# Attention and a mixture of experts on one core: another order and other tile shapes in attention, one output tile that spans the end of each expert's arm, branches announced earlier

## The chip, the core and the metric

The kernel runs on one core of a Trainium2 chip. The core has a matrix engine (TensorE, PE in the profile, with its weight loads as PEld), VectorE (DVE), ScalarE (ACT), GpSimd (POOL) and SyncE (SP, which here only issues transfers). Each engine works through its own instructions in the order in which they were written and waits at semaphores for the others. The metric is the device time of one execution in microseconds (us), lower is better.

## What is computed

`q`, `k`, `v` are 8 batches x 8 heads x 576 positions x 64, all float32. The attention is causal with a decay: each position `s` adds `max(s, 0)` to a running sum, and the difference of two running sums is taken off a score. The heads of a position side by side are a row of 512 numbers, 4608 rows in all. Each row goes to the one expert (of 8) with the largest gate logit.

```python
scores = scale * np.matmul(q, k.transpose(0, 1, 3, 2))
cum = np.cumsum(np.maximum(s, 0.0), axis=-1)
bias = -(cum[:, :, :, None] - cum[:, :, None, :])
scores = np.where(causal, -1000000000.0, scores + np.minimum(bias, 0.0))
attn = np.exp(scores - np.max(scores, axis=-1, keepdims=True))
attn = attn / (np.sum(attn, axis=-1, keepdims=True) + 1e-09)
x = np.matmul(attn, v)            # then rows of 8 heads x 64 = 512
...
e_idx = np.argmax(x @ w_gate, axis=1)
for e in range(E):
    mask = e_idx == e
    h = np.maximum(x[mask] @ w1[e], 0.0)          # 512 -> 1024
    ye = h @ w2[e]                                # 1024 -> 512
    out[mask] = gate_w[mask, None] * eom[mask, e, None] * ye
```

`gate_w` is the softmax weight of the chosen expert, `eom` a sigmoid of a second gate.

## The kernel before

**Attention.** The work goes by pairs of heads: 32 pairs, two heads of 64 side by side in the 128 partitions. Of a pair, q and k are transposed on PE (`trans`, lines 302 and 306) and copied to SBUF (`k_copy`, `q_copy`). The 576 rows of scores are five tiles t = 0..4: four of 128 rows, where tile t needs (t+1)*128 columns, and tile 4, the last 64 rows of both heads, 576 columns. `scores` (line 381) multiplies with 64 rows of the array for each head, so that two heads run side by side. For tile 4 (line 384) each head's 64 rows use one quarter of the array, 64 x 64; the columns are done in two halves of 288, so that two of the four quarters are used. GpSimd writes the decay and the mask into SBUF (`bias`: line 350 for t < 4, 356 and 363 for tile 4, 360 the mask); DVE adds the scores from PSUM and takes the row minimum in one instruction (`least`, line 397, the signs are turned); ACT takes exp and the row sum (`expo`, line 417); PE transposes the result 128 columns at a time (`ptrans`, line 427; the last 64 columns of tile 4 in `ptail`, line 453); ACT or DVE copies it to SBUF (`copy`, lines 310 and 312); PE multiplies by v (`av`, lines 471 and 473, two heads side by side by columns). The result goes through `ocopy` and `xout` (lines 501 and 502: a transpose and the gate logits) and is scaled on DVE (line 514) and stored.

**Banks.** [...] Two are one tile `A` (k, and the product with v); six are one pool, tag `S`, that scores (two banks a tile), transposes, q and `xout` take in turn. A bank is free again when DVE or ACT has read it.

**The order** is made by a planner (`Order`): each piece of work has a place `pos`, an engine, a cost in ns and what it must come after; the planner lets the engines run through these costs and writes each engine's instructions in the order that results. `LAG` is what it adds from an engine's end to another's start, `TURN` what it adds on PE when the shape into which the array is divided changes (0: the whole array; 1: two halves of 64 rows; 2: quarters; 3: two halves of 64 columns). These numbers only set the order.

**Experts.** The last pairs run beside the first expert's early rows (three tiles `ET` of 128 rows gathered from the batches before the last, and two tiles of output `EY`, `early_gemm2`). How many rows an expert has is known only on the chip (`count`, read by every engine in `arm_of`). For each expert there is a switch with one arm per size, 512 to 768 rows in steps of 32 (`front`), and behind the switch code common to all arms (`back`). `hint` lets every engine announce the branch, so that the arm's instructions are fetched ahead. Weights and activations are split into a high and a low float32r part, and a product takes three multiplications (lines 772 and 810). In an arm: h for all eight blocks of 128 (`gemm1`, PSUM tile `ph`, two buffers), then output tile 0 and tiles 4 and above (`gemm2`, PSUM tile `py`, two buffers; 24 multiplications, then DVE scales it into `y`, line 1053, and GpSimd scatters it). A last tile of 32 or 64 rows is done in `gemm2_few` (line 1076). In `back`: output tiles 1, 2, 3 (tile 2 alone for expert 0), between them the transposes of the next expert's gathered rows (`ready`, line 749, with copies `xh` on ACT and `xl` on DVE, line 757), and in the last quarter of tile 3 the hint. If an expert has more than 640 rows, its sixth tile is transposed at the start of the arm (`ready(LT, ...)`).

## Time and profile before

| | |
|---|---|
| median of 3 runs | 912.95 us (912.15 to 914.6) |
| the profiled execution's own time | 906.76 us |
| its span, first to last instruction | 904.9 us |
| mean granted TensorE clock | 0.992 |
| busy: PE, PEld | 858.5 us (95%), 646.5 us (71%) |
| busy: DVE, ACT, POOL | 460.7 us (51%), 444.1 us (49%), 488.1 us (54%) |
| HBM read, written | 102.73 MB, 19.95 MB |

Times in the trace are us from the span's start. A row of a table by stretches has, for each stretch, busy time and number of instructions of each engine, then the granted TensorE clock, the share of the 16 transfer engines in use and GB/s. A row of waits reads: engine and line, `<-` what it waited for, us in total, times, the longest. A row of the chain of waits reads: start, us until the next piece, what ran. A float32 multiplication of two tiles is two instructions (two passes) on PE, a transpose is one.

### The profile page before, as it was taken

The numbers are of one execution on the slowest core, as the hardware profiler recorded it, in microseconds if no ns is written. First come the engines' busy times: TensorE is split into PE (matmuls) and PEld (weight loads), VectorE is DVE, ScalarE is ACT, GpSimd is POOL, SyncE is SP. The second block draws the span as 40 slices with busy tenths as digits, with TensorE's granted clock in tenths as the row PEclk, the third lists the DMA queues.
The fourth block names the chain that finished last, engine by engine and source line by source line (L and its number), as shares of the span: only waits on it lengthen the run. The fifth ranks groups of instructions, "written<-read, shape, count | busy, mean of one in ns | idle before, by whom it ended". The sixth has DMA issues, their size and how long they took to land.

```text
span 904.9 us, 16965 instructions
## 1 busy us (share of the span) xinstructions
PE 858.5 (95%) x5574; PEld 646.5 (71%) x5574; DVE 460.7 (51%) x1274; ACT 444.1 (49%) x1128; POOL 488.1 (54%) x854
## 2 busy tenths in 40 slices
PE   3999999999999999999988989999999999999996
PEld 2656666666666666666877768779779787897985
DVE  4666656575667656676724443536135135352210
ACT  2678777777777778778412514233033042331300
POOL 7685867678686867675551443626135126262401
PEclk9999999999999999999989999999999999999999
DMA  8997687969799697922345361532612615424001
GB/s 184 186 208 178 132 182 147 214 153 204 179 184 207 147 205 160 187 58 73 111 125 170 91 231 57 175 123 70 215 50 59 218 45 157 146 71 137 16 14 51
DMA packets 169449, 124.91 MB, mean 138 GB/s; under 512 B 128650, under 2 KB 147084, under 8 KB 169230
## 3 DMA queue, kind: packets, MB, share of 16 engines
q1 hardware_dynamic: 161150, 100.50, 45.9%
q0 software_dynamic: 8080, 22.08, 8.0%
q8 instruction: 65, 1.06, 0.5%
q14 instruction: 154, 1.26, 0.5%
HBM read 102.73 MB, written 19.95 MB: 136 GB/s over the span
## 4 chain that ended last, share of the span: by engine, by line
PE 79%; issue 9%; POOL 4%; DMA 3%; DVE 2%; SPq 1%; another core or an unknown queue 1%; ACT 0%; POOLq 0%; DVEq 0%; ACTq 0%
PE py L810 17%; PE ph L772 16%; PE PT L427 10%; PE S L381 10%; PE A L473 9%; PE S L384 4%; PE M L501 3%; PE M L502 2%; PE pt L749 2%; PE Aq L306 2%; PE A L306 1%; POOL w L707 1%; PE A L471 1%; PE py L1076 1%; POOL xg L739 1%
## 5 line engine op out<-in xcount | busy, mean ns | idle before, releaser
L810 PE MATMUL py<-w,hh 128*128 128x512 f32 x420 | 133.9, 400 | 7.4 <-DVE y L1053 5.1
L1033 POOL DMA_INDIRECT out_dram<-y,tb x34 | 33.6, 989 | 195.1 <-DVE y L1053 173.5
L427 PE MATMUL PT<-ident,e 128*128 128x128 f32 x768 | 112.8, 280 | 0.6 <-DVE kq L325 0.6
L772 PE MATMUL ph<-xh,w1h 128*128 128x512 f32 (+6 forms) x312 | 104.9, 336 | 6.3 <-issue 4.7
L772 PE MATMUL ph<-xl,w1h 128*128 128x512 f32 (+6 forms) x312 | 103.7, 332 | 4.4 <-DVE xl L757 4.4
L381 PE MATMUL S<-kq 64*128 64x384 f32 (+3 forms) x512 | 104.5, 489 | 1.3 <-ACT kq L323 1.3
L772 PE MATMUL ph<-xh,w1l 128*128 128x512 f32 (+6 forms) x312 | 103.6, 332 | 0.0
L427 PEld LDWEIGHTS PT<-ident,e 128*128 128x128 f32 x768 | 86.4, 144 | 21.4 <-ACT e L417 9.6
L753 ACT CAST xh<-pt 128x512 fp32r<-128x512 f32 x37 | 21.6, 587 | 153.0 <-PE pt L749 147.3
L810 PEld LDWEIGHTS py<-w,hh 128*128 128x128 f32 x420 | 76.7, 189 | 25.5 <-DVE y L1053 7.6
L310 ACT COPY pt<-PT 128x512 f32<-128x512 f32 (+3 forms) x170 | 82.6, 513 | 20.5 <-PE PT L427 19.5
L473 PE MATMUL A<-pt,vraw 128*64 128x448 f32 (+3 forms) x640 | 90.1, 416 | 0.0
L350 POOL TENSOR_SCALAR pbB<-cb,cumt 128x384 f32<-128x384 f32 (+1 forms) x128 | 59.9, 478 | 49.0 <-ACT e L417 33.4
L810 PE MATMUL py<-w,hl 128*128 128x512 f32 x210 | 82.6, 393 | 0.0
L1053 DVE TENSOR_SCALAR y<-py,tb 128x512 f32<-128x512 f32 x33 | 24.8, 751 | 107.3 <-PE py L810 96.2
L721 DVE TENSOR_TENSOR w1l<-w1r,w1h 128x512 fp32r<-128x512 f32 x44 | 50.9, 1156 | 53.1 <-ACT w1h L718 52.9
L473 PEld LDWEIGHTS A<-pt,vraw 128*64 128x64 f32 (+1 forms) x640 | 41.8, 136 | 45.0 <-issue 36.1
L417 ACT ACTIVATE e<-pbA,m 128x512 f32<-128x512 f32 x64 | 46.3, 723 | 56.3 <-DVE m L397 54.2
L772 PEld LDWEIGHTS ph<-xh,w1h 128*128 128x128 f32 x312 | 59.7, 191 | 12.9 <-issue 6.9
L784 DVE SCALAR_TENSOR_TENSOR hl<-ph,hh 128x512 fp32r<-128x512 f32 (+6 forms) x72 | 50.5, 702 | 34.6 <-ACT hh L782 34.5
L417 ACT ACTIVATE e<-pbB,m 128x384 f32<-128x384 f32 (+1 forms) x128 | 64.6, 506 | 5.3 <-DVE m L397 5.3
L772 PEld LDWEIGHTS ph<-xl,w1h 128*128 128x128 f32 x312 | 59.8, 192 | 7.8 <-DVE xl L757 5.2
(171 smaller groups left out, 1907.9 us busy)
## 6 DMA issues: line engine op xcount, KB each, us to landing
cb<-cumd SPq DMA_DIRECT2D x62, 432.0 KB
w1r<-in_moe_w_dram SPq DMA_DIRECT2D x7, 2048.0 KB
w2r<-in_moe_w_dram SPq DMA_DIRECT2D x7, 2048.0 KB
raw<-in_k_dram SPq DMA_DIRECT2D x64, 128.0 KB
raw<-in_q_dram SPq DMA_DIRECT2D x64, 128.0 KB
vraw<-in_v_dram SPq DMA_DIRECT2D x64, 128.0 KB
xd<-x SPq DMA_DIRECT2D x32, 256.0 KB
w1r<-in_moe_w_dram SPq DMA_DIRECT2D x4, 512.0 KB
```

What stands on the lines that cost most here:

```text
L310: nc.scalar.copy(out, in_)
L350: nc.gpsimd.tensor_scalar(pb, st[i]["cb"][:, j, 0:W], 1.0, cumt[:, t, 2 * i + j:2 * i + j + 1], ALU.mult, ALU.add)
L381: nc.tensor.matmul(d["s", t, j][:, 0:width(t)], qt[js, t * P:(t + 1) * P], kt[js, 0:width(t)], start=True, stop=True)
L384: nc.tensor.matmul(d["s", t, n][js, 0:H], d["ql"][js], kt[js, n * H:(n + 1) * H], start=True, stop=True)
L417: nc.scalar.activation(e[:, o:o + W], pbias(i, t, j), AF.Exp, bias=st[i].pop(("m", t, j)), scale=-1.0, accum_out=sums[i % 3][:, j, t:t + 1])
L427: nc.tensor.transpose(p[:, (c * len(g) + n) * P:(c * len(g) + n + 1) * P], st[i][etile(t, j)][:, o:o + P], ident)
L473: nc.tensor.matmul(p[j * D:(j + 1) * D, OB + q0:OB + S], vt[0:kk, j, c, :], pt[0:kk, c, j, q0:S], start=(c == 0), stop=(c == NM))
L721: eng.tensor_sub(w1f("l", f), w1r[:, :, f * P:(f + 1) * P], w1f("h", f).bitcast(F32))
L772: nc.tensor.matmul(p[:, u, 0:W], w1f(a, f)[:, c, :], wt[b_][:, c, us], start=(n == 0), stop=(n == 3 * ND - 1))
L784: nc.vector.scalar_tensor_tensor(lv, pv, 0.0, hv.bitcast(F32), ALU.max, ALU.subtract)
L810: nc.tensor.matmul(p[0:m], wt[a][:, f, sl], w2f(b_, f), start=(f == 0 and n == 0), stop=(f == NF - 1 and n == 2))
L1033: ins = nc.gpsimd.indirect_dma_start(out=dst, out_offset=bass.IndirectOffsetOnAxis(ap=ix, axis=0), in_=y, in_offset=None, bounds_check=dst ...
```

## The change

**Attention, tile 4.** The 64 rows of a head's last tile now take 64 + 256 = 320 columns in each of two halves of the partitions: the lower half the own 64 columns (the only ones that need a mask) and columns 0..255, the upper half columns 192..511, of which the first 64 are masked out. So tile 4 has two parts like the others (j = the head), every one of its four multiplications uses another quarter of the array, and the two heads write different banks. k is laid out with its last 64 columns first, and the running sums get a second layout in DRAM (`cumd`) and in `cb` (1792 instead of 1728 columns). Its row minimum is now taken of two halves: two small copies on ACT (`other_least`) and a minimum on DVE (`both_least`); `sum_move` and `rsum` add the two halves' sums (one more small DVE operation). Two exps of 320 columns take the place of one of 576, two transposes the place of one in `ptail`, two bias operations of 320 the place of one of 576.

**Attention, order.** New places, costs, lags and turn costs; scores only after their bias is written and after the pair before has transposed the same tile. `SLACK` is 40 instead of 250 and the turn cost depends on the shape. The order that the planner then writes is another one. Of the load of the first expert's weights, each piece is issued three pairs earlier.

**Experts.** The first output tile of an expert gets a bank of its own (`pf`). Six of its eight blocks (`FB`) are multiplied in the arm, in pieces ahead of, between and behind the arm's other tiles, the last two behind the end of the arm; `py` has one buffer instead of two, and tile 2 of `back` uses `pf`. The hint stands ahead of tile 3 (of tile 2 for expert 0) instead of in its last quarter; the first expert's hint comes six blocks into the first early output tile. An arm with a sixth tile multiplies the first half of its columns for two blocks ahead.

```diff
-GROUPS = (((3, 0),), ((0, 0), (0, 1)), ((3, 1),), ((2, 0),), ((4, 0),), ((2, 1),), ((1, 0), (1, 1)))
+GROUPS = (((3, 0),), ((0, 0), (0, 1)), ((2, 1),), ((4, 0), (4, 1)), ((1, 0), (1, 1)), ((2, 0),), ((3, 1),))
+BURSTS = ((3,), (0,), (2,), (4,), (1,))
-TURN = 95
+TURN = (95, 200, 125, 150)
-    SLACK = 250
-    LAG = {"PE": 300, "ACT": 250, "DVE": 480, "POOL": 340, "SP": 2300}
+    SLACK = 40
+    LAG = {"PE": 170, "ACT": 370, "DVE": 560, "POOL": 510, "SP": 2300}
...
         for a in range(2):
-            nc.sync.dma_start(cumd[:, a, 0:2, :].rearrange("i j s -> i (j s)"), cum)
-        nc.sync.dma_start(cumd[:, :, 2, :], cum)
+            nc.sync.dma_start(cumd[:, a, 0:2 * S], cum)
+            c4 = cumd[:, a, 2 * S:].rearrange("i (j w) -> i j w", j=2)
+            if a:
+                nc.sync.dma_start(c4, cum[:, H - TL:2 * H])
+            else:
+                nc.sync.dma_start(c4[:, :, 0:TL], cum[:, 2 * H:S])
+                nc.sync.dma_start(c4[:, :, TL:], cum[:, 0:H])
...
-        H = S // 2
-        for n in parts(t):
+        for a in range(1 if t < NM else 2):
             for j in range(2):
                 js = slice(j * D, (j + 1) * D)
...
-                    nc.tensor.matmul(d["s", t, n][js, 0:H], d["ql"][js], kt[js, n * H:(n + 1) * H],
+                    nc.tensor.matmul(d["s", t, j][a * D:(a + 1) * D, 0:W4], d["ql"][js], kt[js, a * H:a * H + W4],
                                      start=True, stop=True)
...
+    def other_least(i):
+        d = st[i]
+        d["mo"] = sm.tile([P, 2], F32, tag="mo", name="mo")
+        for a in range(2):
+            nc.scalar.copy(d["mo"][a * D:(a + 1) * D], d["mt"][(1 - a) * D:(2 - a) * D])
+
+    def both_least(i):
+        d = st[i]
+        nc.vector.tensor_tensor(d["mt"], d["mt"], d["mo"], ALU.min)
...
-        nc.tensor.transpose(p[0:TL, 0:P], st[i]["e4"][:, NM * P:S], ident)
+        for j in range(2):
+            nc.tensor.transpose(p[0:TL, j * P:(j + 1) * P], st[i]["e4"][:, j * W4:j * W4 + TL], ident)
...
-    add("hint", o + 53.0, "PE", 400, hint_first, after=["count", ("g2", EY - 1, 0)])
+    add("hint", o + 43.0, "PE", 400, hint_first, after=["count", ("g2", 0, 1)])
...
+        ahead = range(2) if T > LT and C - c0 > 512 else ()
+        for f in ahead:
+            gemm1(f, c0, C, block(f), 0)
         for f in range(NF):
...
+        first = 0 if e else ET
+        f0 = 2 if few else 0
+        if f0:
+            product2(first, P, firsts[e], range(f0))
         for k, t in enumerate(tiles):
...
+            if k + 1 < len(tiles):
+                product2(first, P, firsts[e], range(f0, f0 + 1))
+                f0 += 1
+        product2(first, P, firsts[e], range(f0, FB))
...
         if e == 0:
-            where = {EY: ((0, 1), (2,), (3,), (4, "hint"))}
+            where = {EY: (("hint", 0, 1), (2,), (3,), (4,))}
         else:
-            where = {1: ((),), 2: ((0,), (1,)), 3: ((2,), (3,), (4,), ("hint",))}
+            where = {1: ((),), 2: ((0,), (1,)), 3: (("hint", 2), (3,), (4,), ())}
+        first = 0 if e else ET
+        product2(first, P, firsts[e], range(FB, NF))
+        result(e, first, P, firsts[e])
```

In the rows that follow, a number behind a tile's name is its buffer, `xN` stands for so many equal instructions, and the size is that of what is written. `S` are scores (`kq` holds k and q), `PT` the transposes of the exp tiles (`e30` and `e31`: tile 3 of head 0 and 1; `e20`, `e21`: tile 2; `e4`, `e1`, `e0`), `A` the product with v or the transpose of k, `M` the output of `xout`.

PE in the middle of attention, from one product with v back to the transposes ahead of it, before:

```order
L427 MATMUL PT_1642<-ident_80,e20_1514 128x128 x3
L302 MATMUL A_1650<-ident_80,raw_1274 128x128
L306 MATMUL A_1650<-ident_80,raw_1274 128x128 x4
L427 MATMUL PT_1663<-ident_80,e4_1544 128x128 x4
L427 MATMUL PT_1677<-ident_80,e21_1553 128x128 x3
L381 MATMUL S_1682<-kq_1458 128x384
L381 MATMUL S_1683<-kq_1458 128x384
L384 MATMUL S_1694<-kq_1458 64x288 x2
L384 MATMUL S_1695<-kq_1458 64x288 x2
L427 MATMUL PT_1707<-ident_80,e1_1557 128x128 x4
L427 MATMUL PT_1722<-ident_80,e30_1622 128x128 x4
L381 MATMUL S_1734<-kq_1458 128x256
```

The same place with the change:

```order
L314 MATMUL A_2077<-ident_80,raw_1658 128x128
L319 MATMUL A_2077<-ident_80,raw_1658 128x128 x4
L448 MATMUL PT_2088<-ident_80,e20_2052 128x128 x3
L448 MATMUL PT_2100<-ident_80,e31_2005 128x128 x4
L396 MATMUL S_2113<-kq_1895 64x320
L396 MATMUL S_2114<-kq_1895 64x320
L396 MATMUL S_2113<-kq_1895 64x320
L396 MATMUL S_2114<-kq_1895 64x320
L393 MATMUL S_2139<-kq_1895 128x512
L393 MATMUL S_2140<-kq_1895 128x512
L393 MATMUL S_2156<-kq_1895 128x128
L393 MATMUL S_2157<-kq_1895 128x128
```

The scores, which stood singly between transposes, now stand together: tile 4, then tiles 3 and 0 of the next pair, in front of the product with v, and tiles 1 and 2 behind it.

PE at the end of an arm of the first expert and the start of the code behind it, before:

```order
L810 MATMUL py<-w_6930,hh 128x512 x2
L810 MATMUL py<-w_6930,hl 128x512
L810 MATMUL py<-w_6935,hh 128x512 x2
L810 MATMUL py<-w_6935,hl 128x512
L1211 UNCONDITIONAL_BRANCH
L852 TENSOR_LOAD rgi
L749 MATMUL pt<-ident,xg 128x128 [waits DMASW3_49,DMASW0_49,PE_49]
L749 MATMUL pt<-ident,xg 128x128 x3
L749 MATMUL pt<-ident,xg 128x128 [waits DMASW5_49,DMASW4_49,DMASW1_49]
L749 MATMUL pt<-ident,xg 128x128 x3
L810 MATMUL py<-w_6843,hh 128x512 [waits DVE_49]
```

With the change:

```order
L1273 UNCONDITIONAL_BRANCH
L877 TENSOR_LOAD rgi
L835 MATMUL pf<-w_7130,hh 128x512 [waits Activation_49]
L835 MATMUL pf<-w_7130,hh 128x512
L835 MATMUL pf<-w_7130,hl 128x512 [waits DVE_49]
L835 MATMUL pf<-w_7160,hh 128x512 [waits Activation_49]
L835 MATMUL pf<-w_7160,hh 128x512
L835 MATMUL pf<-w_7160,hl 128x512 [waits DVE_49]
L881 SWITCH_STRIDE
L881 ISA
L881 BRANCH_PREFETCH_HINT
L774 MATMUL pt<-ident,xg 128x128 [waits DMASW3_49,DMASW0_49,PE_49]
```

Six multiplications into `pf` now stand between the end of the arm and the first transpose, and the announcement of the next branch (`BRANCH_PREFETCH_HINT`) ahead of the transposes instead of behind the last of them.

247 lines of the change are left out of this document (134 added, 113 removed).

## The prediction

> **What bounds the kernel now.** I read the table by stretches first, then who PE waited for, then the chain of waits through one pair of heads, and last the rows around the first expert. By stretches (columns: busy us and count of PE, PEld, DVE, ACT, POOL; clock; transfer share; GB/s), attention, the first expert, the others:
>
> ```profile
> 26.00:420.00 394.00, 393.12 (x2977) 252.08 (x2977) 260.26 (x992) 297.26 (x857) 281.14 (x615) 1.00 0.78 168
> ...
> 464.50:504.50 40.00, 31.49 (x228) 27.46 (x228) 14.34 (x26) 10.96 (x24) 9.82 (x10) 0.87 0.52 170
> 504.50:905.00 400.50, 379.31 (x2057) 323.91 (x2056) 152.11 (x175) 110.02 (x192) 153.58 (x130) 1.00 0.32 106
> ```
>
> In attention PE has work for 393.1 of 394 us; no other engine is above 76%. So in attention only PE's own time counts, and there is no wait to take away: PE is idle for 0.9 us of these 394. In the first expert PE stands still for 8.5 us, in the others and the tail for 21.2. Behind 420 us PE waited for:
>
> ```profile
> PE py L810 <- DVE y L1053: 5.1, 6, 0.8
> PE ph L772 <- issue: 4.7, 3, 4.2
> PE ph L772 <- DVE xl L757: 4.4, 3, 1.8
> PE pt L749 <- DVE xl L757: 4.2, 1, 4.2
> PE py L810 <- issue: 1.7, 1, 1.7
> PE py L810 <- DVE y L1079: 0.6, 1, 0.6
> ```
>
> **Attention, what PE pays for a change of shape.** Parts of the chain through one pair, 177.41 to 190.20 us, 12.79 us long (start, us, what):
>
> ```profile
> 177.41 0.37 PE A L471 x4
> 177.78 2.63 PE A L473 x20
> 180.41 0.23 PE PT L453
> ...
> 180.86 0.44 PE Aq L306 x4
> 181.29 1.06 PE S L381 x4
> 182.35 0.26 PE M L501
> ...
> 184.37 0.42 PE S L381 x4
> ...
> 186.58 0.84 PE S L381 x4
> 187.43 1.12 PE S L384 x8
> 188.54 1.02 PE PT L427 x8
> 189.57 0.63 PE S L381 x4
> ```
>
> The four rows of scores have 128, 256, 384 and 512 columns and take 0.42, 0.63, 0.84 and 1.06 us: 0.21 for each 128 columns, and 0.21 that does not go with the columns. Each of the four follows an operation on the whole array, so that 0.21 is the turn into the half-array shape. A transpose among its like is 0.11 (Aq, 0.44 for 4); the first behind another shape pays more: PT L453 0.23 (+0.12), eight PT 1.02 (+0.14), M, a transpose too, 0.26 (+0.15): 0.13 or a little more. The 0.21 per 128 columns is four passes, two at once, so a pass of 128 columns lasts 0.105. By that A L471 (four passes, two at once) would be 0.21 and is 0.37: turn 0.16. L384 (eight passes of 288 columns at 0.236, two at once) would be 0.95 and is 1.12: turn 0.17.
>
> Counted in the order of instructions up to the first expert's products, PE changes shape 330 times before and 198 times now: into halves by rows 123 and 63, into the whole array 136 and 71, into quarters 32 and 32, into halves by columns 39 and 32. Saved: 60 x 0.21 + 65 x 0.13 + 7 x 0.16 = 22.2 us. Turns from the whole array into quarters and from quarters into halves hardly occur before; I take 0.17 and 0.21. If the 32 turns into quarters cost nothing, that is 5.4 us more saved; if each costs 0.1 more, 3.2 less.
>
> Tile 4 of the scores: eight passes of 320 columns at 0.2625. Four at once 0.53 us, two at once 1.05, before 0.95. That quarters of columns run four at once is shown by the small last tile of the first expert, whose 64 passes of 128 columns would be 6.7 us one by one, 3.4 in twos, 1.7 in fours:
>
> ```profile
> 488.57 1.93 PE py L1076 x64
> ```
>
> With a turn that is fours. Row halves with column halves, four at once, no row shows; the four passes go to four different quarters as those do, so I take 0.53: saved 32 x 0.42 = 13.4. The second tail transpose costs 32 x 0.11 = 3.5. Sum: 22.2 + 13.4 - 3.5 = **32.1 us**, one pair 11.8 instead of 12.8.
>
> **Do the others keep up?** Four pairs, and the first of them:
>
> ```profile
> 151.84:203.00 51.16, 51.16 (x390) 32.81 (x390) 33.01 (x128) 38.74 (x113) 37.00 (x83) 1.00 0.85 184
> 151.84:164.63 12.79, 12.79 (x99) 8.20 (x101) 7.87 (x28) 9.49 (x29) 11.62 (x23) 1.00 1.00 204
> ```
>
> A pair is 8.3 us for DVE, 9.7 for ACT, 9.3 for POOL. Added per pair:
>
> ```profile
> L482 ACT COPY sums<-sums 64x1 f32<-64x1 f32 x32 | 6.1, 189 | 0.8
> L356 POOL TENSOR_SCALAR pbC<-cb,cumtl 128x576 f32<-128x576 f32 (+1 forms) x33 | 24.5, 744 | 0.5 <-ACT e L417 0.4
> L350 POOL TENSOR_SCALAR pbC<-cb,cumt 128x256 f32<-128x256 f32 x64 | 30.0, 480 | 0.0
> 177.34 0.79 ACT L417 ACTIVATE e<-pbC,m 128x576 f32<-128x576 f32 x1
> 178.71 0.50 ACT L417 ACTIVATE e<-pbC,m 128x256 f32<-128x256 f32 x1
> ```
>
> ACT: two small copies (0.38) and two exps of 320 (about 0.56 each, between 256 and 576 columns) for one of 0.79, so +0.7: 10.4 of 11.8, 88%. POOL: two of about 0.53 for one of 0.74 and a mask twice as wide (under 0.1): +0.4, 9.7, 82%. DVE: 64 more columns and one small operation for the sums, +0.2: 8.5, 72%. The longest hand-overs have room. From scores of tile 3 to their transposes PE has tile 0's scores and the product with v, 0.21 + 3.0 us; DVE and ACT need these:
>
> ```profile
> 182.49 0.69 DVE L397 CUSTOM_DVE_ANT_0 pbA<-S,pbA 128x512 f32<-128x512 f32 x1 [1.17 <-POOL pbC L356]
> 183.23 0.72 ACT L417 ACTIVATE e<-pbA,m 128x512 f32<-128x512 f32 x1 [1.98 <-DVE m L397]
> 185.99 0.68 ACT L310 COPY kq<-A 128x640 f32<-128x640 f32 x1
> 187.41 0.62 ACT L323 ACTIVATE kq<-Aq 128x512 f32<-128x512 f32 x1
> ```
>
> 0.69 + 0.72 and hand-overs of 0.05 to 0.15: 1.6 of 3.2. The tightest is k: its transposes stand seven transposes and tile 4's scores (0.77 + 0.70 us) ahead of the next pair's first scores, and the copies of k and q between are 0.68 + 0.62, so PE waits between 0 and 0.3 us a pair, up to 10 us in all. At the end of each of eight batches DVE and POOL also do the routing, inside the 51.16 us of four pairs. I put **5 us** of new waits, bounds 0 and 15. At the start SP issues two more transfers ahead of the next pair's k and q, for which PE waited until 21 us; SP's issues of this kind are 0.6 us each, so **1 us**:
>
> ```profile
> 7.61 0.60 SPq L240 DMA_DIRECT2D cumd<-scr  x1
> 21.04 1.09 PE L306 MATMUL Aq<-ident,raw 128*128 128x128 f32 x4 [2.54 <-DMA raw<-in_q_dram]
> ```
>
> **Experts, four terms.** (1) Bank waits. In `back` the first product waited for DVE's y each time: 5.1 + 0.6 = 5.7 us. Now six multiplications into `pf` (0.23 each, 1.4 us) stand there, more than the 0.84 of the longest wait, and the next users of `py` and `pf` come a tile later: all of it goes. (2) The first arm. The longest `issue` wait, 4.2 us, stands before its first product at 468.64 us, and then PE ran slowly:
>
> ```profile
> 468.64 5.46 PE ph L772 x24
> ...
> 474.76 2.85 PE ph L772 x24
> 469.00:474.30 5.30, 5.30 (x25) 5.23 (x25) 1.24 (x3) 1.02 (x3) 3.71 (x4) 0.50 0.65 192
> ```
>
> The same 24 multiplications took 5.46 us at a granted clock of 0.50 and 2.85 at full speed, 2.6 us lost behind the gap. Announced 30 products (0.23 us each) and two groups of transposes earlier, some 7.7 us, the arm should be there: 4.2 + 2.6 = 6.8 us. If the announcement does not help, nothing. (3) The end of the first arm. DVE did nothing for 5.61 us behind its last y there, and PE's third transpose (`pt`) waited 4.2:
>
> ```profile
> 496.54 1.29 DVE L757 TENSOR_TENSOR xl<-pt,xh 128x512 fp32r<-128x512 f32 x2 [5.61 <-issue]
> ```
>
> The end of this arm is not announced. Nine more multiplications stand between (2.1 us), but DVE has one more y (0.75, like L1053's) ahead of the `xl`: 1.2 us. (4) The sixth tile: `ph` waited 4.4 us for `xl`, 1.63 and 1.76 of it in the two arms that have one (rows below); 24 multiplications of over 300 columns ahead of it (about 0.16 us each) cover 3.8 us: 3.4 us.
>
> ```profile
> 606.47 0.42 PE L772 MATMUL ph<-xl,w1h 128*128 128x336 f32 x1 [1.63 <-DVE xl L757]
> ...
> 672.97 0.43 PE L772 MATMUL ph<-xl,w1h 128*128 128x352 f32 x1 [1.76 <-DVE xl L757]
> ```
>
> Sum 17.1; I take **16**, since the announcements move what other engines fetch too; bounds 9 (terms 1 and 4) and 21 (term 3 whole).
>
> **Sum.** On the profiled execution's own 906.8 us (span 904.9): 906.8 - 32.1 + 5 + 1 - 16 = 864.7. The median of the runs shown is 6.2 above that execution, so **871 us**.
>
> **Rivals.** (a) *Attention becomes bound by the engines that empty the six banks.* A pair uses 21 bank tenancies, each now 3.4 us long on average instead of 3.7, and two tiles' scores in a row take four banks. Against it: DVE and ACT are at 65% and 76% in the row of four pairs. If a pair settles at 12.4 us (half-way back), it costs 32 x 0.6 - 5 = 14 more: 885. [...]
>
> (b) *The quarters do not run four at once:* tile 4 at 1.05 us, 32 x 0.52 = 17 more: 888.
>
> (c) *Transfers.* The first pair of the row above has them at 1.00 with 204 GB/s, the four pairs at 0.85, which is 43.5 us, and cb grows by 64 of 1728 columns. Four new pairs are 47 us, so it fits on average. Where weights load (16 pairs) pairs might stay at 12.8: 16 us, 887.
>
> (d) *Slower: the early announcement is lost.* If what an engine fetched for the branch is thrown away because it goes on through another tile's code first, each of the eight arm entries costs what the first does now, 6.8 us, seven more of them than today: +47.6, against 32.1 - 6 in attention and 5.7 + 3.4 from banks and the sixth tile: 12 slower, 925. It decides from 5.2 us an entry. Against it: the other entries, announced six products (1.4 us) ahead, cost PE 0.5 us together, the 4.7 of three `issue` waits less 4.2. For it: the trace has no branch announced as early as 6 or 7 us ahead. [...]
>
> **Chances.** Forecast 0.62, (a) 0.14, (b) 0.10, (c) 0.06, (d) 0.08. The range 855 to 895: the low end from turns into quarters that cost nothing (5.4), no new waits (5) and 21 in the experts (5); the high end holds (a), (b) and (c) and a part of two of them together. Below 0.3% (2.7 us) this kernel cannot be told from no change. Faster: all but (d) and mixtures, 0.90; same 0.02; slower 0.08.
>
> **What would show it.** In a middle pair of the new chain: 11.8 us between products with v; scores of tile 4 at 0.7 with their turn; 256 and 384 columns together at 1.3 (one turn, not two). PE's wait list in attention below 10 us, k's and q's copies first in it. At the first arm no `issue` gap above 0.5 us and clock 1.00; no row `py <- DVE y`; `ph <- xl` under 1 us. Wrong if pairs stay above 12.3, if `issue` grows at the eight arms, or if PE waits for `raw` or `vraw`.

## The result and the profile after

The changed kernel takes 886.19 us (median of 4, 880.93 to 888.79) against 913.66 us for the kernel before (median of 4, 912.15 to 914.6): ratio 0.9694 with a 95% interval of 0.964 to 0.9747. The forecast was 871 us, within 855 to 895. One execution of one variant below took 1353.57 us at a clock of 0.563 and is left out of that variant's ratio. The profiled execution went from 906.76 to 880.93 us: 25.8 gained, where 42.1 were forecast on that basis.

To see where the 25.8 came from, both profiles are cut within about 1 us of the same four places: the first product of the early rows, the entry into the first arm's `ph`, the second expert's first product, and the end. Table by stretches (us from start to end, length, then busy us and count of PE, PEld, DVE, ACT, POOL; clock; transfer share; GB/s), of before:

```profile
26.00:434.90 408.90, 406.75 (x3091) 261.58 (x3089) 268.28 (x1011) 308.59 (x882) 288.26 (x623) 1.00 0.78 168
434.90:468.00 33.10, 29.00 (x154) 26.41 (x154) 17.61 (x43) 7.90 (x17) 20.05 (x28) 0.99 0.25 73
468.00:504.60 36.60, 31.58 (x228) 27.46 (x228) 12.99 (x24) 10.32 (x22) 7.17 (x8) 0.87 0.51 169
504.60:905.00 400.40, 379.22 (x2056) 323.91 (x2056) 152.07 (x174) 109.92 (x192) 153.58 (x130) 1.00 0.32 106
```

and of the kernel after, with the stretch behind the end of the first arm as a fifth row:

```profile
26.00:425.30 399.30, 381.42 (x3129) 265.07 (x3121) 312.76 (x1142) 293.88 (x918) 301.15 (x656) 1.00 0.80 173
425.30:455.80 30.50, 30.24 (x154) 27.91 (x155) 15.69 (x41) 8.44 (x18) 16.99 (x24) 0.94 0.34 101
455.80:493.60 37.80, 30.66 (x230) 25.97 (x229) 13.46 (x26) 10.35 (x22) 10.04 (x10) 0.91 0.51 172
493.60:880.00 386.40, 375.14 (x2058) 324.53 (x2056) 145.13 (x175) 109.87 (x192) 154.47 (x130) 1.00 0.33 110
477.50:490.00 12.50, 8.25 (x30) 6.88 (x31) 2.60 (x4) 1.76 (x3) 1.78 (x2) 0.73 0.79 294
```

| stage | gained | forecast |
|---|---|---|
| attention | 408.9 - 399.3 = 9.6 | 32.1 - 5 - 1 = 26.1 |
| first expert | (33.1 + 36.6) - (30.5 + 37.8) = 1.4 | terms 2 and 3: 8.0 |
| other experts | 400.4 - 386.4 = 14.0 | terms 1 and 4: 9.1 |

These rows sum to 25.0, since the cuts are rough. Cut at the instructions themselves (early rows from 433.88 and 424.83 us, the second expert from 504.66 and 493.72, the end at 904.9 and 879.1), the stages gain 9.1, 1.9 and 14.9, together 25.8.

By this pair of profiles the experts gave what was forecast, though not where it was forecast, and the whole miss is in attention. The two kernels with one part each, below, divide it differently. In attention PE was busy for 406.75 of 408.9 us before. It is busy for 381.42 of 399.3 us now: its busy time shrank by 25.3 us, and 15.7 of these came back as idle time.

PE's own work did what the sum said. Its timeline in a middle pair of the kernel after (start, us, what), from one product with v to the next:

```profile
232.17 2.80 PE L497 MATMUL A<-pt,vraw 128*64 128x448 f32 x20
234.90 0.88 PE L448 MATMUL PT<-ident,e 128*128 128x128 f32 x6
235.70 1.35 PE L393 MATMUL S<-kq 64*128 64x256 f32 x8
236.98 0.33 PE L526 MATMUL M<-ident,ot 128*128 128x128 f32 x1
...
241.78 0.77 PE L396 MATMUL S<-kq 64*64 64x320 f32 x8
242.48 1.35 PE L393 MATMUL S<-kq 64*128 64x512 f32 x8
243.76 0.44 PE L495 MATMUL A<-pt,vraw 128*64 128x128 f32 x4
244.03 2.80 PE L497 MATMUL A<-pt,vraw 128*64 128x448 f32 x20
```

The pair lasts 244.03 - 232.17 = 11.86 us (11.8 forecast). Tile 4's eight passes take 242.48 - 241.78 = 0.70 us with their turn, so four run at once. The scores of 256 and 384 columns take 236.98 - 235.70 = 1.28 with one turn. But the pair that starts next lasts 14.64, and so it goes at every batch's end: the products with v of the 32 pairs stand 11.8 us apart in between, and 13.4 to 16.1 there. The excess over 11.82 us in pairs 5 to 31 is 19.1 us. In the profile of before the excess over 12.79 was 0.2.

What PE waited for in the kernel after, from 26 to 420 us (engine and line, `<-` what, us in total, times, longest), where before it waited 0.9 us in all:

```profile
PE PT L448 <- DVE m L407: 7.0, 5, 2.5
PE M L526 <- DVE pt L325: 2.5, 3, 1.4
PE PT L448 <- issue: 2.1, 3, 1.2
PE Aq L319 <- DMA raw<-in_q_dram: 1.4, 1, 1.4
```

and behind 425 us:

```profile
PE pf L835 <- issue: 4.3, 1, 4.3
PE ph L797 <- DVE hl L809: 2.6, 2, 1.4
PE py L1113 <- POOL hf L1109: 2.2, 4, 0.8
PE ph L797 <- DVE w1l L746: 1.1, 1, 1.1
PE ph L797 <- ACT xh L778: 0.7, 1, 0.7
PE ph L797 <- DVE xl L782: 0.3, 1, 0.3
```

Of the rows shown before, `py <- DVE y` (5.7 us) and `pt <- DVE xl` (4.2) are gone, `ph <- xl` went from 4.4 to 0.3, and `ph <- issue` (4.7) is gone. In their place stand one gap of 4.3, `pf <- issue`, and some smaller waits for `hl`, `hf` and `w1l`.

**The long pairs.** At the end of a batch GpSimd writes that batch's routing entries with five indirect stores (L655), one behind the other. VectorE in that time, in the kernel after (start, us, what, in brackets the idle time before it):

```profile
249.14 0.42 DVE L407 CUSTOM_DVE_ANT_0 pbC<-S,pbC 128x256 f32<-128x256 f32 x1
...
249.49 0.42 DVE L407 CUSTOM_DVE_ANT_0 pbC<-S,pbC 128x256 f32<-128x256 f32 x1
...
253.07 0.56 DVE L407 CUSTOM_DVE_ANT_0 pbB<-S,pbB 128x384 f32<-128x384 f32 x1 [3.14 <-remote]
```

GpSimd and PE beside it:

```profile
247.20 0.98 POOL L655 DMA_INDIRECT tab<-ent,si  x1 [0.30 <-issue]
...
251.04 0.92 POOL L655 DMA_INDIRECT tab<-ent,si  x1 [0.30 <-issue]
```

```profile
247.56 1.35 PE L393 MATMUL S<-kq 64*128 64x256 f32 x8
...
253.69 0.66 PE L448 MATMUL PT<-ident,e 128*128 128x128 f32 x4 [2.55 <-DVE m L407]
```

The row minimum that starts at 253.07 needs scores that PE finished at 248.91 and a bias that GpSimd wrote from 232.21 to 233.86. Both were there, VectorE had ended its last instruction at 249.92, and it began only when the last store was over (251.96) and 1.1 us more had passed. PE stood still from 251.14 and went on at 253.69, just when this row minimum had been read (253.07 + 0.56): it waited for that PSUM bank. A stop of 1 to 3 us stands at each of the seven batch ends in this profile.

### The profile page after: what moved, and what is told of

Its sections match the earlier page's. It is cut to its first block, busy times and chain, and to the rows that moved or that the text cites. A ratio compares the mean times of both kernels' runs of the same rounds, so it can differ in the third digit from the quotient of the medians.

```text
span 879.1 us, 17334 instructions
## 1 busy us (share of the span) xinstructions
PE 827.5 (94%) x5606; PEld 650.3 (74%) x5606; DVE 496.8 (57%) x1402; ACT 428.2 (49%) x1161; POOL 501.3 (57%) x884
## 3 DMA queue, kind: packets, MB, share of 16 engines
q8 instruction: 64, 1.05, 0.5%
## 4 chain that ended last, share of the span: by engine, by line
PE 50%; issue 21%; DMA 12%; POOL 10%; another core or an unknown queue 3%; DVE 2%; ACT 1%; POOLq 1%; SPq 1%; ACTq 0%
PE PT L448 10%; DMA out_dram<-y,tb 10%; PE A L497 9%; PE S L393 9%; PE ph L797 5%; PE py L835 3%; POOL w L732 3%; PE M L526 3%; PE S L396 2%; PE M L527 2%; POOL out_dram L1064 2%; POOL xg L764 2%; PE Aq L319 2%; POOL w2l L732 1%
## 5 line engine op out<-in xcount | busy, mean ns | idle before, releaser
L448 PE MATMUL PT<-ident,e 128*128 128x128 f32 x768 | 104.2, 277 | 10.1 <-DVE m L407 7.0
L325 DVE COPY pt<-PT 128x512 f32<-128x512 f32 (+3 forms) x157 | 79.1, 528 | 53.5 <-PE PT L448 42.2
L393 PE MATMUL S<-kq 64*128 64x256 f32 (+3 forms) x512 | 87.8, 462 | 1.3 <-ACT kq L336 1.3
L746 DVE TENSOR_TENSOR w1l<-w1r,w1h 128x512 fp32r<-128x512 f32 x45 | 48.5, 1079 | 58.3 <-ACT w1h L743 52.2
L835 PE MATMUL py<-w,hh 128*128 128x512 f32 x240 | 76.2, 399 | 0.0
L393 PEld LDWEIGHTS S<-kq 64*128 64x128 f32 x512 | 46.4, 189 | 36.5 <-issue 19.2
L732 POOL TENSOR_TENSOR w<-w2r,w 128x512 fp32r<-128x512 f32 x45 | 58.4, 1309 | 8.9 <-ACT w2h L729 3.8
L370 POOL TENSOR_SCALAR pbA<-cb,cumt 128x512 f32<-128x512 f32 x64 | 43.6, 691 | 33.0 <-ACT e L435 13.2
L743 ACT CAST w1h<-w1r 128x512 fp32r<-128x512 f32 x48 | 29.8, 620 | 66.4 <-issue 52.8
```

The lines of the kernel that those rows point to most:

```text
L325: nc.vector.tensor_copy(out, in_)
L370: nc.gpsimd.tensor_scalar(pbias(i, t, j), cb[:, c0 + j * w:c0 + j * w + W], 1.0, cumt[:, t, 2 * i + j:2 * i + j + 1] if t < NM else cumtl[ ...
L393: nc.tensor.matmul(d["s", t, j][:, 0:width(t)], qt[js, t * P:(t + 1) * P], kt[js, TL:TL + width(t)], start=True, stop=True)
L448: nc.tensor.transpose(p[:, (c * len(g) + n) * P:(c * len(g) + n + 1) * P], st[i][etile(t, j)][:, o:o + P], ident)
L732: eng.tensor_sub(w2f("l", f), w2r[:, f], w2f("h", f).bitcast(F32))
L746: eng.tensor_sub(w1f("l", f), w1r[:, :, f * P:(f + 1) * P], w1f("h", f).bitcast(F32))
```

## Experiments

Kernels of one set ran on one chip, beside runs of the kernel before on it. Before took 913.8 us on the first chip, 913.2 on the second and 905.1 on the third; so ratios are compared, and times only within a set.

### The two parts apart (first chip)

One kernel has the new attention with the experts' code of before; the other has the new experts' code with the attention of before.

```diff
-    add("hint", o + 43.0, "PE", 400, hint_first, after=["count", ("g2", 0, 1)])
+    add("hint", o + 53.0, "PE", 400, hint_first, after=["count", ("g2", EY - 1, 0)])
...
-        f0 = 2 if few else 0
-        if f0:
-            product2(first, P, firsts[e], range(f0))
```

> The kernel before with the change's attention part alone (tile 4, order, loads); the experts, their banks and announcements as before. Theory A (the loss is in attention): in the changed kernel's profile a pair takes 11.8 us as forecast, but every fourth pair 13.4 to 16, and the first early product of the experts comes only 9.7 us earlier (425.6 instead of 435.3). So this kernel is 8 to 12 us faster than before: 902 to 906. Rival B (the attention part gains its forecast 26 us and the two parts cost each other something at the hand-over): 885 to 891.

Measured: 894.89 us, ratio 0.9807 (0.9767 to 0.9846), 18.9 us gained, which lies between theory A and rival B. The long pairs are there, with an excess of 19.0 us. The entry into the first arm has its gap (4.2 us, `issue`), while the end of the arm has none (PE waits 3.1 us for `xl` there).

```diff
-GROUPS = (((3, 0),), ((0, 0), (0, 1)), ((2, 1),), ((4, 0), (4, 1)), ((1, 0), (1, 1)), ((2, 0),), ((3, 1),))
+GROUPS = (((3, 0),), ((0, 0), (0, 1)), ((3, 1),), ((2, 0),), ((4, 0),), ((2, 1),), ((1, 0), (1, 1)))
...
-    SLACK = 40
+    SLACK = 250
```

> The kernel before with the experts' part alone (own bank for the first tile, blocks around the end of the arm, earlier announcements, sixth tile in halves); attention as before. Theory A: what the two profiles show behind 435.3 and 425.6 us, 25.8 - 9.7 = 16 us faster: 896 to 900. Rival B (the expert part's gain depends on the new attention order): less than 10 us faster, 904 or more.

Measured: 903.47 us, ratio 0.9884 (0.9846 to 0.9922), 10.3 us gained, where theory A had 16. The two parts add to 29.2 us, the whole change gave 27.5: they do not disturb each other by more than these measurements tell.

So by parts both fall short: attention 18.9 of 26.1, the experts 10.3 of 16. From the first product of the early rows to the last instruction it is 471.0 us in the profile of before, 465.8 with the attention part alone, 461.7 with the experts' part alone and 454.3 with both. Some 5 us of what the table credits to the experts therefore come with the new attention; by what way is open.

This profile settled something else. Its attention is instruction for instruction that of before, and yet VectorE has a wait that the profile of before does not have at all (its waits from 26 to 420 us):

```profile
DVE pbC L397 <- remote: 16.7, 6, 4.5
```

Its pairs at batch ends last 14.4 us instead of 12.9, an excess of 7.8 us, and its last product with v is at 436.19 instead of 427.92 us. So the stop is not new. The kernel before, whose attention this is, has it on this chip, and pays some 8 us for it. The profile of before comes from an execution without it. Its 906.76 us are not among the times listed with the result, and on which chip it ran is not known.

### The stores not one behind the other (first chip)

The last four stores of batches 0 to 5 are issued one at a time, each behind a bias of one of the next two pairs. Nothing else moves.

```diff
-        steps += [(f"enter{t}", "POOL", 1280, lambda t=t: enter(z.si, z.ent, t), ("weight", "places"))
+        steps += [(f"enter{t}", "POOL", 1280, lambda t=t: enter_later(b, t, lambda: enter(z.si, z.ent, t)), ("weight", "places"))
...
+    def enter_later(b, t, fn):
+        if t == 0 or b > B - 3:
+            return fn()
+        later.setdefault((NPAIR * b + 8 + (t - 1) // 2, TILES[3 * ((t - 1) % 2)]), []).append(fn)
```

> The changed kernel, and of the five indirect stores of routing that GpSimd issues back to back at a batch's end, the last four of batches 0 to 5 are issued one at a time behind later bias work of the next two pairs; every other instruction of every engine stands as it stood. Theory P (while GpSimd issues these stores VectorE's next instruction does not start; PE then waits for VectorE): the six long pairs shrink from 13.4 to 14.7 us to about 12.5, 8 to 14 us in all, to 872 to 878, and the seventh, where the stores are still together, stays at 14 to 16. Rival R (VectorE is late because of routing's own 5 us of instructions in that pair): the long pairs stay, time within 2 us of the changed kernel's 886.

Measured: 875.09 us, ratio 0.9572 (0.953 to 0.9614): 11 us less than the kernel after, 10.4 less than the next kernel of the same set, which times like it. VectorE's stops at batch ends are gone: a single store from 256.28 to 257.30 lets it start an instruction at 257.06. Pairs at those batch ends last 12.9 us (one 13.4), the others 11.8; the seventh batch, left as it was, has 17.2. What remains at each is a wait of VectorE's routing for GpSimd's gate logits `lg`, which now come later (timeline of VectorE in this kernel):

```profile
227.53 0.20 DVE L591 TENSOR_REDUCE mx<-lg 128x5 f32<-128x40 f32 x1 [2.17 <-POOL lg L553]
```

It costs 1.05 us in five of the six pairs and 1.6 in one. So five stores in a row are what VectorE stands still for on this chip, and single ones are not.

### The first announcement late again (first chip)

The first expert's branch is announced late again, in the last early output tile (six multiplications, 1.4 us, sooner than before the change); the rest is the kernel after.

```diff
-    add("hint", o + 43.0, "PE", 400, hint_first, after=["count", ("g2", 0, 1)])
+    add("hint", o + 53.0, "PE", 400, hint_first, after=["count", ("g2", EY - 1, 1)])
```

> The changed kernel with the announcement of the first expert's branch put back to where it stood before, half an early output tile (12 products) ahead of the branch. Both theories expect the gap at the entry (4.2 us) and the slow clock behind it back, 4 to 7 us. Theory J (the early announcement is what takes PE's code behind the arm's end away, the 4.3 us at 477 us): that gap goes, VectorE's wait there returns instead, net 0 to 4 us slower than the changed kernel. Rival K (PE fetches behind this arm whatever the announcement): the gap of 4.3 us stays, 5 to 8 us slower.

Measured: 885.44 us, ratio 0.9703 (0.9652 to 0.9755), no difference from the kernel after; the 5 to 8 us of rival K did not come, though its gap did. PE's waits behind 420 us:

```profile
PE pf L835 <- issue: 3.6, 1, 3.6
PE ph L797 <- issue: 3.2, 1, 3.2
```

The gap at the entry is back (3.2 us), so the early announcement does take it away. The gap at the end of the arm (3.6) is there as well, so it is not the early announcement that makes it. From PE's announcement to the arm's first product it is 5.0 us here (454.5 to 459.5) and 4.5 in before (464.1 to 468.6); in the kernel after it is 10.8 (445.2 to 455.9), with other work between and no gap. From the first `ph` to the next expert's h it is 71.6 us here, 68.9 in the kernel after: the early announcement is worth 2.7 us in the profile, not the 6.8 of the forecast, and the times do not show it.

### More stores, or as much other work of GpSimd (second chip, then third)

If the stores themselves stop VectorE, five more of them elsewhere should stop it again, and other work of GpSimd should not. One kernel writes each batch's entries a second time into a table that nothing reads; another does fifteen small GpSimd operations into a tile that nothing reads. First both stood behind the bias of tile 4 (`TILES[3]`) two pairs later.

```diff
+    def spare_later(b, z):
+        if b <= B - 3:
+            later[NPAIR * b + 9, TILES[3]] = [lambda t=t: spare(z.si, z.ent, t) for t in range(NT)]
```

> The changed kernel with five more indirect stores on GpSimd, back to back, for each of batches 0 to 5, of the same rows into a table that nobody reads, behind a bias operation about one and a half pairs after the real ones, where no routing runs; all else stands as it stood. Theory P (VectorE is held while such stores come back to back): six more long pairs of 13.4 to 14.7 us, 9 to 17 us slower than the changed kernel's 886: 895 to 903. Rival R (routing's own instructions on VectorE make the long pairs): no new long pairs, 886 to 890.

> The same places, but fifteen additions of 128 columns on GpSimd (about 5 us, the time of five stores) instead of the five stores. Theory P: what holds VectorE is the store, so pairs stay near 11.8 us and the kernel within 4 us of 886. Rival Q (it is GpSimd's time: its bias work comes late and VectorE waits for that): the same new long pairs as with the stores, 895 to 903.

Measured: 905.8 us (0.992, 0.9891 to 0.9949) with the stores, 899.75 us (0.9869, 0.9819 to 0.9919) with the arithmetic. Against the 886.2 us of the kernel after these are 19.6 and 13.6 more, and both are more than theory P had. The arithmetic costs nearly as much as the stores, for a reason of its own: both stand ahead of the gate logits of the next batch, and VectorE waited for those 17.5 us in the kernel with the arithmetic, 5.8 in the one with the stores. So the times do not tell stores from other work of GpSimd. The profiles do, at the place itself. VectorE and GpSimd there, first with the stores (VectorE's line is 408 in this kernel, the added store's 664), then with the arithmetic:

```profile
231.33 0.42 DVE L408 CUSTOM_DVE_ANT_0 pbC<-S,pbC 128x256 f32<-128x256 f32 x1 [0.20 <-PE S L394]
...
232.24 0.92 POOL L664 DMA_INDIRECT tab<-ent,si  x1 [0.30 <-issue]
...
234.42 0.56 DVE L408 CUSTOM_DVE_ANT_0 pbB<-S,pbB 128x384 f32<-128x384 f32 x1 [2.66 <-remote]
```

```profile
226.62 5.63 POOL L664 TENSOR_SCALAR spare<-ident 128x128 f32<-128x128 f32 x15
...
230.41 0.42 DVE L407 CUSTOM_DVE_ANT_0 pbC<-S,pbC 128x256 f32<-128x256 f32 x1
...
230.75 0.56 DVE L407 CUSTOM_DVE_ANT_0 pbB<-S,pbB 128x384 f32<-128x384 f32 x1
```

With the stores VectorE stands still for 2.66 us, though its bias was written by 221.26 us and its scores were done by 230.49. With as long a run of arithmetic it goes on at once. The six pairs with the added stores last 13.2 to 16.0 us, the same six with the arithmetic 11.8 to 11.9; the arithmetic's long pairs come one later, at the wait for the gate logits. So on this chip it is the stores, in a place without routing, as theory P said.

To free both from the gate logits, they were put one pair earlier, and ran on the third chip:

```diff
-            later[NPAIR * b + 9, TILES[3]] = [lambda t=t: spare(z.si, z.ent, t) for t in range(NT)]
+            later[NPAIR * b + 8, TILES[3]] = [lambda t=t: spare(z.si, z.ent, t) for t in range(NT)]
```

> The changed kernel with five more stores, back to back, for batches 0 to 5, this time one pair behind the real ones instead of two: before, the added work also stood ahead of the next batch's gate logits on GpSimd, so that VectorE's routing waited for these (17.5 us in six waits with the additions). Theory P (stores back to back hold VectorE, whatever its data): six new long pairs, VectorE idle in them with its inputs written and scores done; 8 to 16 us slower than the changed kernel's 886, 894 to 902. Rival R: within 4 us of 886.

> The same place one pair behind the stores, with fifteen additions of 128 columns (about 5 us of GpSimd) instead of five stores. Theory P: GpSimd is late by 5 us and catches up, its bias is written a pair ahead; 886 to 891, pairs there below 12.8 us. Rival Q (any 5 us of GpSimd do the same): as with the stores.

Measured: 889.1 us (0.9832, 0.9801 to 0.9863) and 882.56 us (0.9752, 0.9726 to 0.9778), on a chip where before takes 905.1. Here neither the added stores nor the real ones stop VectorE, and that 889.1 lies within rival R's 4 us of 886 says nothing, since it is another chip. The instructions of the rows shown above, in the kernel with more arithmetic, whose five real stores stand in a row as in the kernel after:

```profile
251.13 0.42 DVE L407 CUSTOM_DVE_ANT_0 pbC<-S,pbC 128x256 f32<-128x256 f32 x1
...
251.47 0.42 DVE L407 CUSTOM_DVE_ANT_0 pbC<-S,pbC 128x256 f32<-128x256 f32 x1
...
251.81 0.56 DVE L407 CUSTOM_DVE_ANT_0 pbB<-S,pbB 128x384 f32<-128x384 f32 x1
```

```profile
249.89 0.98 POOL L655 DMA_INDIRECT tab<-ent,si  x1 [0.30 <-issue]
...
253.73 0.92 POOL L655 DMA_INDIRECT tab<-ent,si  x1 [0.30 <-issue]
```

The `pbB` instruction follows the `pbC` at once, under the same stores. So the expected stop failed to come. What the added work costs here it costs by order: the routing of the next batch waits for the gate logits behind it (20.1 us in total with the stores, 14.6 with the arithmetic, as VectorE's waits show), and one pair a batch lasts 15.8 to 16.4 us with the stores, 13.1 to 17.0 with the arithmetic. Every profile taken on the first two chips that has five stores in a row in attention shows stops there, and none of the four taken on the third does; what differs between the chips is not known.

It does agree with the times of before: 913 us on the chips with the stop and 905 on the one without, 8 us apart, and 8 us is what before's attention lost in its pairs on the first chip. The profile of before, with 906.76 us and no stop, looks like those of the third chip, where before takes 902 to 908 us; whether it ran on that chip or on one with the stop is open.

### The tile that spans the end of the arm (second and third chip)

With the stores apart as above, all eight blocks of the first expert's tile are multiplied in the arm, so that behind its end PE begins with transposes, as before. The hint stands behind these transposes.

```diff
-        product2(first, P, firsts[e], range(f0, FB))
+        product2(first, P, firsts[e], range(f0, FB if e else NF))
```

> The kernel with the stores apart, and for the first expert all eight blocks of the tile multiplied in the arm, so that behind the arm's end PE's first work is two groups of transposes, as before the change; the next branch is announced behind them. To be compared with the kernel with the stores apart (875). Theory K (PE itself waits for its code behind the arm): the gap of 4.2 us stays and stands ahead of the transposes; within 2 us of 875. Rival S (PE's code is there, and its first product behind the arm waits for a semaphore of ScalarE or VectorE, which wait for their code): no gap ahead of the transposes, a wait for xl of 2 to 4 us behind them, 872 to 875.

Measured: 872.37 us, ratio 0.9565 (0.9519 to 0.961). PE's timeline at the end of the arm, first of the kernel after, then of this one:

```profile
477.06 0.40 PE L835 MATMUL pf<-w2h,hl 128*128 128x512 f32 x1
481.75 1.19 PE L835 MATMUL pf<-w,hh 128*128 128x512 f32 x2 [4.29 <-issue]
```

```profile
471.08 0.39 PE L835 MATMUL pf<-w,hl 128*128 128x512 f32 x1
474.33 1.06 PE L774 MATMUL pt<-ident,xg 128*128 128x128 f32 x8 [2.87 <-issue]
```

The gap stands ahead of the transposes too. It belongs to no particular instruction. The reading taken here is that PE waits for its own code behind the end of the arm. The transfers of instructions on one queue fit it (queue, kind, packets, MB, share). In the kernel after none ran from 462 to 477.4 us, when PE was in the arm's last part, and one while PE stood still, from 477.4 to 481.8:

```profile
q8 instruction: 1, 0.02, 1.4%
```

That this queue is PE's, and that the gap is a wait for code, is inferred from such times.

In the last variant the small tile of the first expert's arm comes last instead of first, the rest as in the kernel just shown.

```diff
-        f0 = 2 if few else 0
+        f0 = (2 if e else NF) if few else 0
...
-                product2(first, P, firsts[e], range(f0, f0 + 1))
+                product2(first, P, firsts[e], range(f0, min(f0 + 1, NF)))
```

> The kernel with the whole tile in the first expert's arm, and there the small tile (32 rows) last, as before the change, instead of between the blocks; stores apart, branch announced early. Theory F (with the small tile last, PE's code behind the arm is fetched some 5 us ahead, as it was in the kernel before and in the one with the attention part alone): no gap of PE behind the arm; PE waits for xl instead, 3 to 4 us; within 3 us of the 872 of the kernel with the whole tile in the arm. Rival E (the early announcement of the branch costs the fetch): the gap of 2.9 us or more stays.

Measured: 871.69 us, ratio 0.9639 (0.9613 to 0.9665) on the third chip. As theory F said, PE's gap at the end of the arm is gone (0.12 us), and its instruction transfer lies ahead of it, between 459 and 465.4 us. But the wait for `xl` is 6.3 us instead of the 3 to 4 expected (PE's row, then VectorE's):

```profile
474.19 1.12 PE L774 MATMUL pt<-ident,xg 128*128 128x128 f32 x4 [6.27 <-DVE xl L782]
```

```profile
472.79 0.75 DVE L1101 TENSOR_SCALAR y<-pf,tb 128x512 f32<-128x512 f32 x1 [7.02 <-DMA out_dram<-y,ixf]
```

PE does two groups of transposes and six multiplications and then waits 6.27 us for VectorE, which has done nothing for 7.02 us behind the end of the arm. Not all of that can be a wait for code. The trace has VectorE's branch at 465.43 us and its next instruction, a load of registers, at 470.33: 4.9 us. From there to 472.59 it waits for the small tile's scatter, which landed at 472.56; this is the `DMA out_dram<-y,ixf` of the row. With the small tile last, its scatter is issued late (466.05), and the first `y` behind the arm waits for it. So up to 2 us of the 6.27 come from the new order of tiles and not from the code.

In the kernel before it was VectorE too, with its 5.61 us, of which 5.5 lie between its branch (490.61) and the same load (496.13). In thirteen profiles this stretch of VectorE's is 3.9 to 6.1 us, also where PE has a gap of its own: in the kernel after it runs from 476.65 to 482.04 (5.4 us), beside PE's gap (4.29 us). So VectorE comes late behind this arm in every version, and PE too where the small tile does not stand last.

### All stores apart, and sooner (second and third chip)

The seventh batch's stores were also put one by one, among the work of the eighth.

```diff
+        if t == 0 or b == B - 1:
+            return fn()
+        key = LAST_BATCH[t - 1] if b == B - 2 else ("b", NPAIR * b + 8 + (t - 1) // 2, TILES[3 * ((t - 1) % 2)])
```

> As the kernel with the stores apart, and the seventh batch's last four stores also one at a time, between GpSimd's bias and weight work in the last pairs. Theory P: the last long pair (17.2 us) shrinks by 2 to 3 us and the first early product comes 2 to 3 us earlier: 871 to 874. Rival: the early gather then waits for the later stores, 875 or more.

Measured: 876.45 us, ratio 0.9606 (0.9562 to 0.9649). With the seventh batch's stores apart as well nothing more is gained, as the rival had it; why is open.

Then the four stores were put closer together, behind three biases of one pair and the first of the next, so that the gate logits need not wait for them, together with the tile in the arm.

```diff
-        later.setdefault((NPAIR * b + 8 + (t - 1) // 2, TILES[3 * ((t - 1) % 2)]), []).append(fn)
+        later.setdefault([(NPAIR * b + 8, 3), (NPAIR * b + 8, NM), (NPAIR * b + 8, 2), (NPAIR * b + 9, 3)][t - 1], []).append(fn)
```

> The kernel with the whole tile in the arm and the stores apart, but the four stores behind four bias operations of one pair, so that they are done before the next batch's gate logits; with the earlier spacing one pair a batch stays at 12.85 us, since VectorE's routing waits 2.2 us for these logits on GpSimd. Theory P: those six pairs fall to 11.8 us, 6 us faster than 872: 865 to 868. Rival: with four stores in one pair VectorE is held again, 872 or more.

Measured: 868.52 us, ratio 0.9591 (0.9562 to 0.9619), the lowest time of all. The reason expected did not hold: pairs at batch ends still last 12.9 us (one 13.4), and VectorE still waits for the gate logits 9.9 us in six places. The 3.2 us less than the variant with the small tile last, in the same set, are about the difference at the end of the arm, where PE waits 3.0 us in this one and 6.3 in that.

Three versions lie with their whole interval below that of the change (0.964 to 0.9747): stores apart (0.9572), with the tile in the arm (0.9565), and with the stores sooner (0.9591). For the first two, on chips where before takes the same 913 us, this means faster than both kernels. The third ran on the chip where before is faster itself, and the kernel after was not run there.

## Why the prediction was right or wrong

**The time of 871 us was 15 too low; the range held it, and that was luck.** The upper half of the range stood for rivals (a), (b) and (c); what filled it was another wait. PE's own work in attention was forecast right: the turns, four quarters at once, the pair of 11.8 us. Rivals (a) and (b) are out by the rows of the middle pair: no pair settled at 12.4, and tile 4 takes 0.70 us; but (a) was nearer than its 0.14, as the largest of PE's waits in attention, `PT <- DVE m` (7.0 us), is one for banks. Rival (c) is out too: apart from 1.4 us for `raw` at the start, no transfer stands among PE's waits of attention.

**The step that failed is the 5 us of new waits of PE (bounds 0 and 15).** They came to 18.9 in the pairs (19.1 less the 0.2 of before). "The tightest is k" was wrong in kind: no row of PE's waits in attention names the copies of k or q. The largest is for `m`, VectorE's row minimum, and behind it stands a VectorE that does nothing. The working counted the routing at the end of a batch into the mean of four pairs, and a mean says nothing of five stores in a row; besides, the profile it was read from shows no stop. For attention the sum then closes: 32 pairs of 12.79 - 11.82 = 0.97 us are 31.0, less 18.9 in the long pairs and 2.9 at the start is 9.2, and the stretch shows 9.6.

**The 6.2 us between the profile of before and its median were the same thing, unread.** They were carried over as a constant. The kernel with the experts' part alone shows what they may be made of: 7.8 us of stops at batch ends, in an attention that had 0.2 us in the profile. Whether the profile of before came from another chip or from a quicker execution on the same one is not known. Stores apart gave 11 us back.

**A second step failed beside it: VectorE's load.** The forecast added 0.2 us to a pair for VectorE, 8.5 of 11.8, and 0.7 for ACT. Four pairs of the kernel with its stores apart, whose VectorE has the same instructions as the kernel after, in the columns of the tables by stretches:

```profile
203.17:251.99 48.82, 47.56 (x398) 33.34 (x396) 40.11 (x149) 36.10 (x116) 39.17 (x88) 1.00 0.92 194
```

VectorE has 40.11 us in four pairs, 10.0 each, where it had 33.01 before: 82% instead of 65%. ACT has 36.1, less than the 38.7 of before. The new order has moved copies from ACT to VectorE. Groups of VectorE's instructions in two pairs, of the kernel after (220.36 to 244.03) and of before (177.41 to 203):

```profile
L325 DVE COPY pt<-PT 128x512 f32<-128x512 f32 (+3 forms) x10 | 5.0, 527 | 3.0 <-PE PT L448 2.9
```

```profile
L312 DVE COPY pt<-PT 128x256 f32<-128x256 f32 (+1 forms) x4 | 2.0, 490 | 1.1 <-PE PT L427 1.1
```

Ten copies instead of four. Each engine's count of instructions by line would have shown it before any run. VectorE therefore has 1.8 us a pair left to catch up behind a stop, instead of 4.5, and the banks that it empties come late. That this is why a stop costs the new order more than the old (in the rows above 2.55 of 3.14 us) is argued from these loads; no run changed the load alone.

The instruction that stood still for 3.14 us has one operand in SBUF and one in PSUM (`pbB`, `S`). The one with the same operands at 251.81 us on the third chip has no idle time ahead of it, under the same five stores. The stores are shown to be the cause on the second chip (2.66 us of standstill with them, none with 5.63 us of arithmetic); the mechanism is open.

**The start** cost 1.5 us at the second wait for `raw` (21.04 to 22.50) and 1.4 in a third, 2.9 instead of 1.

**Experts, term by term** (the 16 was the second term that came short, 10.3 by the experts' part alone). Terms 1 and 4, 9.1 forecast: no `py <- DVE y` is left, and `ph <- xl` is 0.3. PE's idle time behind the first expert is 386.4 - 375.1 = 11.3 us, before 400.4 - 379.2 = 21.2, so 9.9 of the 14.0 are waits. The other 4.1 are shorter busy time for the same number of multiplications, which was not worked out; two products right behind a wait show 0.73 us instead of 0.62, which is a part of it. From the second expert's first product to the end the experts' part alone gains 8.0 us (400.2 to 392.2) and the attention part alone 2.5 (397.7).

Terms 2 and 3, 8.0 forecast, 1.4 gained (1.9 by the instructions themselves): both mechanisms were half right. The gap at the first entry went as foreseen, 4.2 us to none. Behind it PE waits for `w1l` and `hl` instead, 1.07 and 1.41 us in the first arm, and the clock's fall came along to the next gap: the stretch from 477.5 to 490 us has 0.73. "The end of this arm is not announced" was said, but taken as VectorE's fetch, which nine multiplications of PE would cover. They did not: PE then stood still for 4.3 us itself, by the reading above for its own code. The two runs with the tile inside the arm show that the wait stays when the multiplications go (2.87 us), and that PE waits for VectorE instead (6.3, up to 2 of it for a scatter) when it has no gap of its own (0.12).

**Rival (d), slower,** is out. No arm's entry costs PE more than 1.1 us, and the only `issue` gap among the experts is at the end of the first arm, which is not an entry. The first arm was announced 10.8 us ahead, with other tiles' code between, and PE had no gap at its entry; the late announcement brought 3.2 us back. Where nothing announced the branch, at the end of the arm, PE stood still for 4.3 us.

## What to carry to other kernels

When a change takes away the slack of a stage, look for the instants at which an engine does something once every few rounds, not at its mean. Here five stores in a row, which cost the kernel before some 8 us unseen in its profile, cost the new one more, and spreading them, with no other change, gave 11 us. When the profiled execution of a kernel is quicker than its other runs, ask what those runs have that the profile lacks, before it is carried over as a constant; and compare kernels on the same chip. Behind the end of an arm that nothing announces, look at every engine's first instruction, not only at the one that is waited for: here VectorE came 4 to 6 us late in every version, and moving PE's work across the join only changed who waited beside it.

## What the runs showed of the hardware

VectorE does nothing for 1 to 3 us (4.5 once) while GpSimd issues five indirect stores back to back, with its inputs complete where they were followed (253.07 us above, and 234.42 in the kernel with more stores), on two chips; on a third it runs through them (251.81 us above, no idle time). A single store has no such effect (from 256.28 to 257.30 us with the stores apart; VectorE starts at 257.06), and neither has 5.6 us of GpSimd arithmetic (from 226.62; VectorE starts at 230.41 and 230.75). The kernel before takes 913 us on the two and 905 on the third.

PE's clock falls for a few us, at places that differ from one profile to the next. Of 10-us stretches ahead of 420 us, those from 20, 150 and 250 us lie below 1.00 in the kernel with the attention part alone (0.66, 0.83, 0.83), those from 20 and 300 in the one with the late announcement (0.83 both), and none in the kernel after, all with the same attention code. In the profile of the kernel after the clock is 0.50 from 426.2 to 429.6 us and from 480.9 to 487.6. The stretch from 420 to 430 us has the first of these, behind waits of 0.3 to 0.7 us (length, busy us and count of the five engines, clock):

```profile
420.00:430.00 10.00, 8.10 (x46) 7.19 (x45) 7.17 (x13) 6.06 (x12) 7.31 (x9) 0.83 0.73 260
```

A clock of 0.83 over 10 us loses some 1.7 us. The four executions of the kernel after have a mean clock of 0.993 at 880.93 us and 0.984 at 883.8 to 888.8, which would fit four or five such falls more (an estimate: 0.009 of 880 us is 8 us); the profile of only one was at hand. In the profile of before, where PE waits 0.9 us in attention, the clock is 1.00 up to the first arm. So a wait of PE seems able to cost more than its length (behind the gap of 4.2 us in before, 24 multiplications took 5.46 us instead of 2.85); that is the author's estimate, and no run changed the waits alone.

Into an arm that it announced 10.8 us ahead PE goes without a gap (first product at 455.91 us), though other tiles' code runs in between; announced late, the arm's first product came 4.5 and 5.0 us behind the announcement, with gaps of 4.2 and 3.2 us. PE's gap behind the first expert's arm is 0.12 us with the small tile last in the arm, and with it earlier 4.29 (the kernel after), 3.6 (the late announcement) and 2.87 (the tile in the arm); on the third chip, with the tile in the arm in both, it is 0.12 against 3.0.
